# A hand-written issue order rearranged over the first two tiles of a fused window attention and squared-ReLU feed-forward kernel

## The chip, the cores and the metric

The kernel runs on one core of one Trainium2 chip. The metric is the device time of one execution in microseconds (us). Before the change three runs took 849.35, 850.06 and 850.16 us (median 850.06).

## The reference

Eight batches of eight heads, 576 positions each, head size 64. A query sees itself and the 63 positions before it. The result, brought to 4608 tokens of 512 numbers, goes through a two-layer feed-forward block. All of it is float32.

```python
scores = scale * np.matmul(q, k.transpose(0, 1, 3, 2))
mask = (rel >= 0) & (rel < window)          # window = 64
attn = softmax(np.where(mask, scores, -1e9))
x = np.matmul(attn, v)                      # -> (4608, 512)
h = x @ w_in                                # (512, 2048)
r = np.maximum(h, 0.0)
return (r * r) @ w_out                      # (2048, 512)
```

## The kernel before, in words

The 4608 tokens are cut into 12 tiles of 384 tokens. Attention is done in sections: each tile has three sections of four items, an item being a block of 64 queries of four heads. The feed-forward block is done in steps: one step is a tile with one of the 16 blocks of 128 hidden units. Each float32 operand of the feed-forward block is split into a high and a low part, and each product is made of three matmuls (high by high, high by low, low by high).

The first part of the program, through tile 1 and beyond it, is issued in an order that is written out by hand: the string `order`, a list of short tokens. A loop takes token after token and records its instructions; each of the five engines then executes its own instructions in exactly the recorded order and waits with a semaphore where data is missing. So an instruction that waits holds up everything behind it on its engine. After the string, a planner orders the rest; the change does not touch that.

A token is a letter with a number, sometimes with an engine letter behind it (d VectorE, a ScalarE, p GpSimd). The number of an attention token is its section (0 to 2 belong to tile 0, 3 to 5 to tile 1), that of a weight token the weight block, that of a feed-forward token the step. Steps 0 to 4 are tile 0 with weight blocks 0 to 4, steps 5 to 9 are tile 1 with the same blocks. The profile calls TensorE PE, VectorE DVE, ScalarE ACT, GpSimd POOL and SyncE SP.

Loading and turning:
- L, N: DMAs of q and k of batch 0 and 1 (L185). v: DMAs of v (L157). w: two DMAs of one weight block (L104, L105). All are issued by SP, in the order of the tokens. SP has eight completion semaphores in turn, so a DMA is issued only after the one eight places ahead has landed.
- T, U: PE transposes of q and k of batch 0 and 1 (L196). t, u: the copies out of PSUM (L202). U0 to U3 share one PSUM bank, so each waits for the copy of the one before.
- K: matmuls of the identity by itself that nobody reads (L512); K4 is four of them.

Splitting a weight block (two scratch buffers `a`, used in turn):
- a: ScalarE (L118). b: two DVE operations (L120, L121). c: DVE (L123). d: DVE (L125). h: high part, ScalarE (L129). l: low part, DVE (L132). They follow from each other, except that c and d need the weights' words too.

A section of attention, in the order of its dependences:
- S: scores on PE (L235). o: copy on ScalarE (L243). s: masked copy on DVE (L252, L253). z: maximum on DVE (L255). y: its scaling on POOL (L257). e, f: the two halves of the exponentials on ScalarE (L263, four pairs of instructions each). k: a small sum on POOL (L266). R: reciprocal on DVE (L269). m: the multiplication by it on POOL or DVE (L272). X: transposes on PE (L276). x: masked copy on DVE (L280). V: values on PE (L298). H: high part of the result (L313, DVE or ScalarE). Q: low part, DVE (L315).

A feed-forward step:
- M: 12 matmuls (L404). r: ReLU on ScalarE (L413). p: square (L416 on ScalarE). g: high part, ScalarE (L421). G: low part, DVE (L423). O: nine matmuls (L446). All M share one PSUM bank.

M0 needs the three sections of tile 0 (their H and Q) and weight block 0; M5 needs those of tile 1.

Of the kernel before, what the change touches and what calls it, by code (L numbers as in the profile page):

```python
# [29 lines left out]
def window_attention_relu2_ffn(ctx: ExitStack, tc: tile.TileContext, q, k, v, w_in, w_out, out):  # L30
# [457 lines left out]
    order = """
        L0 L1 w0 L2 T0 v0 T1 t0a t1d S0 w1 T2 o0a T3 K5 t2d v1 s0 t3d a0 z0 S1 L3 y0 b0 f0 N0 T4 K3 c0 o1a L4
        t4a s1 T5 K5 e0 w2 d0 t5a N1 k0 z1 h0 S2 R0 y1 v2 m0d e1 l0 X0 K6 o2a x0 a1 v3 s2 V0 f1 b1 H0a k1 T6 K4  # L490
        w3 z2 R1 y2 t6d m1p v4 f2 Q0 T7 X1 c1 t7a U0 e2 x1 S3 u0a k2 d1 V1 o3a T8 v5 H1a R2 s3 m2p t8a T9 a2 Q1
        X2 t9d z3 h1 U2 K2 w4 b2 y3 u2a U1 K4 f3 w5 x2 u1a w6 c2 U3 e3 S4 w7 l1 u3a V2 k3 o4a v6 R3 H2a s4 m3p
        Q2 S5 a3 z4 X3 o5a b3 M0 y4 f4 x3 e4 c3 V3 r0 k4 d2 p0a M1 v7 H3a g0 R4 Q3 m4p h2 s5 X4 r1 G0 p1a z5 O0
        g1 x4 y5 e5 G1 V4 d3 f5 O1 v8 l2 H4a k5 h3 R5 Q4 m5p M2 a4 l3 w8 w9 X5 r2 b4 a5 M3 w10 x5 p2a w11 g2 c4
        r3 V5 w12 p3a G2 g3 w13 d4 O2 w14 G3 h4 H5d O3 w15 l4 q0 Q5 a6 M4 b5 b6 r4 M5 p4a c5 g4 q1 c6 r5 M6 p5a
        G4 g5 d6 O4 r6 d5 h6 G5 p6a M7 h5 g6 l5 O5 r7 G6 a7 l6 p7a O6 b7 g7 a8 G7 M8 c7 b8 O7 r8 p8a d7 g8 M9 G8
        h7 c8 O8 r9 l7 p9a g9 d8 a9 M10 G9 h8 b9 O9 r10 l8 p10a g10 c9 a10 B0 M11 G10 b10 O10 r11 p11a d9 g11 B1
        M12 G11 h9 c10 O11 r12 l9 p12a g12 d10 a11 B2 M13 G12 h10 b11 O12 r13 l10 p13a g13 c11 a12 B3 M14 G13
        b12 O13 r14 p14a d11 g14 B4 M15 G14 h11 c12 O14 r15 l11 p15a g15 d12 a13 B5 M16 G15 h12 b13 O15 r16 l12
        p16a g16 c13 a14 B6 M17 G16 b14 O16 r17 p17a d13 g17 B7 M18 G17 h13 c14 O17 r18 l13 p18a g18 d14 a15 B8  # L500
        M19 G18 h14 b15 O18 r19 l14 p19a g19 c15 B9 M20 G19 D0 O19 r20 p20a d15 q2 g20 M21 G20 h15 D1 O20 r21
        l15 p21a g21 q3 G21 M22 O21 r22 p22d g22 G22 M23 D2 O22 r23 p23d q4 g23 M24 G23 Z22 W22 O23 r24 p24d g24
        G24 S6 M25 o6a D3 q5 s6 O24 r25 z6 p25a y6 g25 f6 G25 S7 O25 e6 o7d s7 v9 k6 z7 M26 R6 y7 m6p f7 D4 X6
        e7 q6 S8 x6 r26 k7 V6 R7 o8a p26d m7p M27 H6a s8 g26 Q6 z8 X7 r27 G26 y8 M28 p27a x7 e8 D5 O26 g27 f8
        G27 q7 V7 r28 k8 R8 p28a m8p S9 g28 H7d M29 G28 Q7 o9d v10 X8 r29 s9 M30 p29a x8 g29 z9 v11 V8 r30 D6 y9
        f9 M31 p30d H8a e9 Q8 O27 k9 R9 m9p G29 O28 g30 r31 p31d X9 G30 g31 O29 x9 D7 G31 M32 O30 r32 p32d g32
        M33 G32 O31 r33 Z31 W31 p33d g33 G33 q8 q9"""
# [586 lines left out]
```

## Time and profile before

| | |
|---|---|
| median of three runs | 850.06 us |
| the profiled execution | 849.04 us, of which the profile's span is 846.9 us |
| PE busy | 828.6 us, 98% of the span |
| DVE busy | 592.3 us, 70% |
| ACT busy | 407.9 us, 48% |
| POOL busy | 182.8 us, 22% |

The span is the time from the first to the last instruction of the profiled execution; all times in rows are counted from its start. A row of the timeline gives an instruction's start, its length, the engine, the line of the kernel, the operation, what it writes and reads, how many were merged, and in brackets the idle time of the engine before it with what ended it. Engines write their results a little later than they can take the next instruction, so neighbouring rows overlap by some 0.1 us on DVE and ACT and by some 0.2 us on PE. A float32 matmul outside the feed-forward block is recorded twice, so four of them show as eight.

### The profile page before, as it was taken

How to read it: one execution, taken by the hardware profiler on the slowest of the kernel's cores; microseconds unless marked ns; L12 is line 12 of the kernel's file. 1: busy time of each engine (PE TensorE's matmuls, PEld its weight loads, DVE VectorE, ACT ScalarE, POOL GpSimd, SP SyncE). 2: the span in 40 equal slices, each digit the busy share in tenths (PEclk: the TensorE clock that was granted, in tenths of full speed). 3: DMA queues.
4: the chain of work that ended last, by engine and by line, in shares of the span. 5: the costliest groups of instructions: out<-in, count | busy, mean ns of one | idle time of the engine just before them, and what ended most of it. 6: DMA issues, size and time to landing. Idle time of an engine off the chain costs nothing.

```text
span 846.9 us, 17709 instructions
## 1 busy us (share of the span) xinstructions
PE 828.6 (98%) x6754; PEld 760.7 (90%) x6754; DVE 592.3 (70%) x889; ACT 407.9 (48%) x1127; POOL 182.8 (22%) x239
## 2 busy tenths in 40 slices
PE   6799999999999999999999999999999999999998
PEld 5688999899999999999999999999999999999997
DVE  5899996656766867867777765688755668544553
ACT  5786874645546554554452354353455324222221
POOL 1220003204557520311230121141112131010110
PEclk9999999999999999999999999999999999999999
DMA  9989966537699884999897786999775555776411
GB/s 216 214 264 359 277 275 117 94 103 175 169 198 265 210 178 112 296 250 209 185 320 247 172 221 158 280 233 264 219 233 154 194 191 180 239 258 212 134 68 74
DMA packets 273011, 173.92 MB, mean 205 GB/s; under 512 B 190496, under 2 KB 239648, under 8 KB 270880
## 3 DMA queue, kind: packets, MB, share of 16 engines
q1 hardware_dynamic: 272928, 172.80, 73.5%
q8 instruction: 53, 0.87, 0.4%
q14 instruction: 30, 0.25, 0.1%
HBM read 138.15 MB, written 34.60 MB: 204 GB/s over the span
## 4 chain that ended last, share of the span: by engine, by line
PE 86%; SPq 4%; DMA 3%; DVE 3%; issue 2%; ACT 1%; POOL 0%; DVEq 0%; POOLq 0%
PE banks L991 29%; PE banks L910 26%; PE banks L446 11%; PE banks L404 11%; PE banks L235 3%; PE banks L298 3%; PE banks L276 2%; DMA w<-in_moe_w_out_dram 1%; SPq L185 1%; DVE a L123 1%; SPq L157 1%; DMA raw<-in_q_dram 1%; DMA w<-in_k_dram 1%; SPq L104 1%; DVE g L423 1%
## 5 line engine op out<-in xcount | busy, mean ns | idle before, releaser
L991 PE MATMUL banks<-w 128*128 128x512 f32 x1152 | 257.5, 380 | 0.0
L991 PEld LDWEIGHTS banks<-w 128*128 128x128 f32 x1152 | 215.7, 189 | 28.4
L404 PE MATMUL banks<-x,w 128*128 128x384 f32 x768 | 137.1, 328 | 1.9 <-ACT r L413 1.4
L446 PE MATMUL banks<-w,g 128*128 128x512 f32 x576 | 136.2, 382 | 0.1
L404 PEld LDWEIGHTS banks<-x,w 128*128 128x128 f32 x768 | 126.6, 189 | 6.1 <-ACT r L413 3.3
L910 PE MATMUL banks<-x,w 128*128 128x384 f32 x768 | 130.3, 326 | 0.0
L936 POOL TENSOR_TENSOR g<-g 128x384 f32<-128x384 f32 x64 | 58.3, 914 | 324.5 <-ACT g L947 309.6
L910 PEld LDWEIGHTS banks<-x,w 128*128 128x128 f32 x768 | 125.6, 189 | 0.0
L446 PEld LDWEIGHTS banks<-w,g 128*128 128x128 f32 x576 | 106.3, 189 | 14.5 <-DVE g L423 1.3
L263 ACT ACTIVATE sel<-sel,nm 128x64 f32<-128x64 f32 x272 | 90.8, 336 | 25.0 <-DVE nm L257 23.1
L910 PE MATMUL banks<-w 128*128 128x384 f32 x576 | 100.7, 329 | 0.0
L999 DVE TENSOR_TENSOR w<-w,banks 128x512 f32<-128x512 f32 x72 | 49.5, 687 | 69.1 <-PE banks L991 68.2
L910 PEld LDWEIGHTS banks<-w 128*128 128x128 f32 x576 | 93.8, 189 | 1.9
L981 ACT CAST w<-w 128x512 fp32r<-128x512 f32 x48 | 29.8, 620 | 72.9 <-PE banks L991 72.9
L413 ACT ACTIVATE r<-banks 128x384 f32<-128x384 f32 x64 | 31.4, 491 | 66.8 <-PE banks L404 66.3
L981 ACT CAST w<-g 128x512 fp32r<-128x512 f32 x48 | 29.7, 621 | 62.1 <-PE banks L991 60.1
L272 POOL TENSOR_TENSOR sel<-sel,nm 128x512 f32<-128x512 f32 x33 | 36.1, 1094 | 107.4 <-ACT g L947 51.7
L263 ACT ACTIVATION_READ_ACCUMULATOR sel<-sel,nm 128x1 f32 x272 | 51.1, 188 | 0.0
L423 DVE TENSOR_TENSOR g<-r,g 128x384 fp32r<-128x384 f32 x64 | 37.5, 586 | 18.0 <-ACT g L421 10.2
L929 DVE SCALAR_TENSOR_TENSOR w<-w 128x384 f32<-128x384 f32 x64 | 47.1, 736 | 1.8
L280 DVE TENSOR_TENSOR pt<-banks,masks 128x1024 f32<-128x1024 f32 x33 | 40.3, 1220 | 10.9 <-PE banks L276 10.9
L535 POOL TENSOR_TENSOR a<-w 128x256 f32<-128x256 f32 x28 | 25.0, 908 | 105.4 <-DVE w L132 79.6
(103 smaller groups left out, 982.1 us busy)
## 6 DMA issues: line engine op xcount, KB each, us to landing
w<-mixed SPq DMA_DIRECT2D x128, 256.0 KB, 5.2
w<-kept SPq DMA_DIRECT2D x64, 512.0 KB, 7.3
w<-kept SPq DMA_DIRECT2D x96, 256.0 KB, 5.9
kept<-w SPq DMA_DIRECT2D x16, 1024.0 KB, 8.5
vt<-in_v_dram SPq DMA_DIRECT2D x144, 64.0 KB, 3.1
w<-in_moe_w_in_dram SPq DMA_DIRECT2D x16, 512.0 KB, 7.5
w<-in_moe_w_out_dram SPq DMA_DIRECT2D x16, 512.0 KB, 8.4
raw<-in_q_dram SPq DMA_DIRECT2D x112, 72.0 KB, 3.2
```

The costliest lines, as they stand in the source:

```text
L263: act.activation(sels[i][:, w, hd], sels[i][:, w, hd], AF.Exp, bias=nms[i][:, n], scale=SCALE, accum_out=sums[i][:, n])
L272: (dve if eng == "d" else pool).tensor_tensor(p, p, rs[i][:, :, None].broadcast_to([P, SW * 2, QB]), ALU.mult)
L280: dve.tensor_tensor(pts[i].rearrange("p (w n) q -> p w n q", n=2), ps_t[i][:, :, None, :].broadcast_to([P, SW, 2, P]), masks.rearrange("p ...
L404: pe.matmul(h_ps, lhsT=weights(kk, part), rhs=in_turn(x[xx][:, kk // 2, kk % 2]), start=n == 0, stop=n == 3 * NK - 1)
L423: dve.tensor_tensor(gs[n][1], rg.pop(n), gs[n][0].bitcast(F32), ALU.subtract)
L446: pe.matmul(acc(t, tb), lhsT=gg[:, ts], rhs=in_turn(weights(part)), start=f == 0 and n == 0, stop=f == NF - 1 and n == 2)
L910: pe.matmul(ps[:, :TT], lhsT=w[:, part, kk * P:(kk + 1) * P], rhs=in_turn(x[:, xx, kk]), start=n < 4 and m == 0, stop=m == 5, skip_group_c ...
L929: plan("dve", 0.57, lambda: dve.scalar_tensor_tensor(x(), x(), 0.0, x(), ALU.max, ALU.mult), [], keys)
L936: plan("pool", 0.95, lambda: pool.tensor_tensor(x(), x(), x(), ALU.mult), [], keys)
L981: plan("act", 0.62, lambda: act.copy(high(c), src()), g_keys, [kh], 0, freed("hi") if new else [])
L991: pe.matmul(ps, lhsT=gg[:, m // 2, m % 2], rhs=in_turn(wo_slot(w[m])[:, part]), start=m == 0 and n == 0, stop=m == 3 and n == 2)
L999: plan("dve", 0.72, lambda: dve.tensor_tensor(by_half(parts(tb)), by_half(parts(tb)), ordered(ps), ALU.add), [key], [kp])
```

## The change

The string `order` is written anew from shortly before the third weight block (w2) is used to shortly before the fourth step. The instructions are the same, with two exceptions: of ten idle matmuls (K4, K2, K4) seven are left (K4, K3), and the high part of section 5 (H5) is made by ScalarE instead of DVE.

```diff
-        t4a s1 T5 K5 e0 w2 d0 t5a N1 ... K6 o2a x0 a1 v3 s2 V0 ...
-        X2 t9d z3 h1 U2 K2 w4 b2 y3 u2a U1 K4 f3 w5 x2 u1a w6 c2 U3 e3 S4 w7 l1 u3a V2 k3 o4a v6 R3 H2a s4 m3p
-        Q2 S5 a3 z4 X3 o5a b3 M0 y4 f4 x3 e4 c3 V3 r0 k4 d2 p0a M1 v7 H3a g0 R4 Q3 m4p h2 s5 X4 r1 G0 p1a z5 O0
...
+        t4a s1 T5 K5 e0 w2 d0 t5a N1 ... K6 o2a x0 a1 w3 s2 V0 ...
+        X2 t9d z3 K3 x2 y3 l1 f3 a2 w4 b2 U2 u2a V2 U1 w5 H2a u1a U3 w6 u3a Q2 S4 w7 c2 o4a d2 M0 a3 s4 z4 r0 e3
+        v6 b3 S5 y4 k3 R3 m3p o5a X3 p0a c3 f4 M1 x3 V3 g0 G0 e4 k4 O0 v7 H3a r1 R4 Q3 h2 m4p s5 X4 p1a l2 z5 g1
...
```

In words: the DMAs of weight block 3 (w3) are issued ahead of those of v3. Ahead of the first operation on weight block 2 (a2 on ScalarE, b2 on DVE) now stand h1 and f3 on ScalarE, x2 and l1 on DVE. V2 moves up to the place right behind U2, and M0 to the place behind S4, ahead of S5 and X3. The other half of the exponentials of section 3, e3, moves down behind r0. x3 and V3 now follow M1 instead of preceding it, and M2 stands ahead of V4 and O1 instead of behind them. l2 moves up from behind d3 to the place ahead of z5; r2 and p2a move up ahead of H4 and a4.

TensorE before, from the wait for batch 1's second load (`w_209` is what N0 and N1 load, `w_354` and `qk_78` are turned q and k, `w_111`, `sel_79` and `pt_80` belong to attention, `x1_318` is tile 0's attention result, `w_248` and `w_433` are the split weight blocks 0 and 1). The rows are U2, K2, U1, K4, U3, V2, S5, X3, M0 and V3:

```order
L196 MATMUL banks_75<-ident_85,w_209 128x64 x4
L512 MATMUL banks_75<-ident_85 128x128 x2
L196 MATMUL banks_75<-ident_85,w_209 128x128 x4
L512 MATMUL banks_75<-ident_85 128x128 x4
L196 MATMUL banks_75<-ident_85,w_209 128x64 x4
L298 MATMUL banks_75<-pt_80,vt_77 64x128 x8
L298 MATMUL banks_75<-pt_80,vt_77 64x64 x16
L235 MATMUL banks_75<-w_354 64x128 x16
L276 MATMUL banks_75<-ident_85,w_111 128x128 x4
L404 MATMUL banks_75<-x1_318,w_248 128x384 x12
L298 MATMUL banks_75<-w_111,vt_77 64x128 x8
```

After the change the same stretch of TensorE, to V3 as well (tile 0's result is now called `x1_317`, weight block 1 `w_426`):

```order
L512 MATMUL banks_75<-ident_85 128x128 x3
L196 MATMUL banks_75<-ident_85,w_209 128x64 x4
L298 MATMUL banks_75<-pt_80,vt_77 64x128 x8
L298 MATMUL banks_75<-pt_80,vt_77 64x64 x16
L196 MATMUL banks_75<-ident_85,w_209 128x128 x4
L196 MATMUL banks_75<-ident_85,w_209 128x64 x4
L404 MATMUL banks_75<-x1_317,w_248 128x384 x12
L235 MATMUL banks_75<-w_354 64x128 x16
L276 MATMUL banks_75<-ident_85,w_111 128x128 x4
L404 MATMUL banks_75<-x1_317,w_426 128x384 x12
L298 MATMUL banks_75<-w_111,vt_77 64x128 x8
```

V2 (`pt_80`) stands right behind U2 and the idle matmuls ahead of it, M0 (`w_248`) stands ahead of S5 and X3, and M1 (`w_426`) stands between X3 and V3. S4 is left out of both pieces.

ScalarE before, over sections 3 and 4. The rows with `w_111` are f3 and e3, those with `w_354` the copies u1, u3, the CAST H2, the L118 row a3 (`w_329` is the raw weight block 3), the row with x8 is f4 and e4 together, L413 is r0:

```order
L263 ACTIVATE w_111,nm_81<-w_111,nm_81 128x64 x4
L202 COPY w_354<-banks_75 128x4x128
L263 ACTIVATE w_111,nm_81<-w_111,nm_81 128x64 x4
L202 COPY w_354<-banks_75 128x4x64
L243 COPY sel_79<-banks_75 128x512
L313 CAST x1_318<-banks_75 128x2x2x128
L118 ACTIVATE a_84<-w_329 128x1024
L243 COPY sel_79<-banks_75 128x512
L263 ACTIVATE sel_79,nm_81<-sel_79,nm_81 128x64 x8
L413 ACTIVATE r_82<-banks_75 128x384
```

ScalarE after, from o4 on (`w_291` is the raw weight block 3): a3, r0, e3, o5, p0 and the first half of section 4's exponentials.

```order
L243 COPY sel_79<-banks_75 128x512
L118 ACTIVATE a_84<-w_291 128x1024
L413 ACTIVATE r_82<-banks_75 128x384
L263 ACTIVATE w_111,nm_81<-w_111,nm_81 128x64 x4
L243 COPY sel_79<-banks_75 128x512
L416 ACTIVATE r_82<-r_82 128x384
L263 ACTIVATE sel_79,nm_81<-sel_79,nm_81 128x64 x4
```

The second half of section 3's exponentials has moved from the place behind u1 to the place behind r0, which reads what M0 wrote.

VectorE before, around section 3's reciprocal (the first L269 row, R3); behind it stand s4 and Q2:

```order
L132 TENSOR_TENSOR w_433<-a_84,w_433 128x2x512
L269 RECIPROCAL nm_81<-nm_81 128x8
L252 COPY_PREDICATED sel_79<-late_90,neg_92 128x2x128
L253 COPY_PREDICATED sel_79<-late_90,banks_75 128x2x128
L315 TENSOR_TENSOR x1_318<-banks_75,x1_318 128x2x2x128
```

VectorE after, around the same reciprocal; behind it stands c3, then x3 (L280) and G0 (L423):

```order
L253 COPY_PREDICATED sel_79<-late_90,banks_75 128x2x128
L255 TENSOR_REDUCE nm_81<-sel_79 128x8
L120 TENSOR_SCALAR a_84<-a_84 128x1024
L121 TENSOR_SCALAR a_84<-a_84 128x1024
L269 RECIPROCAL nm_81<-nm_81 128x8
L123 SCALAR_TENSOR_TENSOR a_84<-w_291,a_84 128x1024
L280 TENSOR_TENSOR w_111<-banks_75,masks_91 128x1024
L423 TENSOR_TENSOR g_83<-r_82,g_83 128x384
```

R3 has moved behind b3, and the neighbour behind it is no longer a masked copy but c3, which reads the weights' words and the scratch buffer, both in SBUF.

More of the change, by code (lines that the diff above doesn't have):

```diff
@@ L489, in window_attention_relu2_ffn @@
         L0 L1 w0 L2 T0 v0 T1 t0a t1d S0 w1 T2 o0a T3 K5 t2d v1 s0 t3d a0 z0 S1 L3 y0 b0 f0 N0 T4 K3 c0 o1a L4
-        t4a s1 T5 K5 e0 w2 d0 t5a N1 k0 z1 h0 S2 R0 y1 v2 m0d e1 l0 X0 K6 o2a x0 a1 v3 s2 V0 f1 b1 H0a k1 T6 K4
-        w3 z2 R1 y2 t6d m1p v4 f2 Q0 T7 X1 c1 t7a U0 e2 x1 S3 u0a k2 d1 V1 o3a T8 v5 H1a R2 s3 m2p t8a T9 a2 Q1
-        X2 t9d z3 h1 U2 K2 w4 b2 y3 u2a U1 K4 f3 w5 x2 u1a w6 c2 U3 e3 S4 w7 l1 u3a V2 k3 o4a v6 R3 H2a s4 m3p
-        Q2 S5 a3 z4 X3 o5a b3 M0 y4 f4 x3 e4 c3 V3 r0 k4 d2 p0a M1 v7 H3a g0 R4 Q3 m4p h2 s5 X4 r1 G0 p1a z5 O0
@@ L494, in window_attention_relu2_ffn @@
[L494 to L507, printed above, removed]
+        t4a s1 T5 K5 e0 w2 d0 t5a N1 k0 z1 h0 S2 R0 y1 v2 m0d e1 l0 X0 K6 o2a x0 a1 w3 s2 V0 f1 b1 H0a k1 T6 K4
@@ new lines, in window_attention_relu2_ffn @@
+        v3 z2 R1 y2 t6d m1p v4 f2 Q0 T7 X1 c1 t7a U0 e2 x1 S3 u0a k2 d1 V1 o3a T8 v5 H1a R2 s3 m2p t8a T9 Q1 h1
+        X2 t9d z3 K3 x2 y3 l1 f3 a2 w4 b2 U2 u2a V2 U1 w5 H2a u1a U3 w6 u3a Q2 S4 w7 c2 o4a d2 M0 a3 s4 z4 r0 e3
+        v6 b3 S5 y4 k3 R3 m3p o5a X3 p0a c3 f4 M1 x3 V3 g0 G0 e4 k4 O0 v7 H3a r1 R4 Q3 h2 m4p s5 X4 p1a l2 z5 g1
+        y5 x4 M2 e5 G1 V4 d3 f5 O1 v8 r2 H4a k5 h3 R5 Q4 m5p p2a a4 l3 g2 w8 w9 X5 b4 a5 M3 w10 x5 G2 w11 c4 r3
+        V5 w12 p3a O2 g3 w13 d4 w14 G3 H5a h4 O3 w15 l4 q0 Q5 a6 M4 b5 b6 r4 M5 p4a c5 g4 q1 c6 r5 M6 p5a G4 g5
@@ new lines, in window_attention_relu2_ffn @@
+        d6 O4 r6 d5 h6 G5 p6a M7 h5 g6 l5 O5 r7 G6 a7 l6 p7a O6 b7 g7 a8 G7 M8 c7 b8 O7 r8 p8a d7 g8 M9 G8 h7 c8
+        O8 r9 l7 p9a g9 d8 a9 M10 G9 h8 b9 O9 r10 l8 p10a g10 c9 a10 B0 M11 G10 b10 O10 r11 p11a d9 g11 B1 M12
+        G11 h9 c10 O11 r12 l9 p12a g12 d10 a11 B2 M13 G12 h10 b11 O12 r13 l10 p13a g13 c11 a12 B3 M14 G13 b12
+        O13 r14 p14a d11 g14 B4 M15 G14 h11 c12 O14 r15 l11 p15a g15 d12 a13 B5 M16 G15 h12 b13 O15 r16 l12 p16a
+        g16 c13 a14 B6 M17 G16 b14 O16 r17 p17a d13 g17 B7 M18 G17 h13 c14 O17 r18 l13 p18a g18 d14 a15 B8 M19
@@ new lines, in window_attention_relu2_ffn @@
+        G18 h14 b15 O18 r19 l14 p19a g19 c15 B9 M20 G19 D0 O19 r20 p20a d15 q2 g20 M21 G20 h15 D1 O20 r21 l15
+        p21a g21 q3 G21 M22 O21 r22 p22d g22 G22 M23 D2 O22 r23 p23d q4 g23 M24 G23 Z22 W22 O23 r24 p24d g24 G24
+        S6 M25 o6a D3 q5 s6 O24 r25 z6 p25a y6 g25 f6 G25 S7 O25 e6 o7d s7 v9 k6 z7 M26 R6 y7 m6p f7 D4 X6 e7 q6
+        S8 x6 r26 k7 V6 R7 o8a p26d m7p M27 H6a s8 g26 Q6 z8 X7 r27 G26 y8 M28 p27a x7 e8 D5 O26 g27 f8 G27 q7
+        V7 r28 k8 R8 p28a m8p S9 g28 H7d M29 G28 Q7 o9d v10 X8 r29 s9 M30 p29a x8 g29 z9 v11 V8 r30 D6 y9 f9 M31
@@ L508, in window_attention_relu2_ffn @@
+        p30d H8a e9 Q8 O27 k9 R9 m9p G29 O28 g30 r31 p31d X9 G30 g31 O29 x9 D7 G31 M32 O30 r32 p32d g32 M33 G32
+        O31 r33 Z31 W31 p33d g33 G33 q8 q9"""
     ps_f = {}
```

## Prediction

> **What bounds the kernel now.** I read first who waited for whom on TensorE (PE), from 66 us to the end (us in total, times, longest).
>
> ```profile
> PE banks L404 <- ACT r L413: 1.2, 2, 0.6
> PE banks L298 <- DVE pt L280: 0.3, 1, 0.3
> ```
>
> These are all the waits in 780 us: behind 66 us PE runs without a hole. So whatever the rearranged stretch does to the start of step 4 (M4, 63.10 below), the end of the program takes over one for one. The stretch itself, in the table by windows (length, then busy us and number of instructions of PE, its weight loads, DVE, ACT and POOL, granted clock, DMA share, GB/s):
>
> ```profile
> 30.00:66.00 36.00, 31.38 (x393) 27.51 (x394) 32.36 (x43) 29.06 (x79) 6.45 (x9) 0.95 0.86 242
> ```
>
> No engine is full here; DVE comes nearest, with 36.00 - 32.36 = 3.64 us idle. What counts is the chain from engine to engine. The timeline of PE shows where it breaks.
>
> ```profile
> 29.91 0.66 PE L276 MATMUL banks<-ident,w 128*128 128x128 f32 x4
> 32.84 0.25 PE L196 MATMUL banks<-ident,w 64*128 64x64 f32 x1 [2.28 <-DVE a L120]
> 33.29 0.40 PE L196 MATMUL banks<-ident,w 64*128 64x64 f32 x3 [0.20 <-DMA w<-in_k_dram]
> 38.28 1.08 PE L298 MATMUL banks<-pt,vt 64*64 64x128 f32 x48
> 40.12 1.10 PE L235 MATMUL banks<-w 64*64 64x128 f32 x32 [0.76 <-ACT x L313]
> 41.15 0.65 PE L276 MATMUL banks<-ident,w 128*128 128x128 f32 x4
> 41.56 2.20 PE L404 MATMUL banks<-x,w 128*128 128x384 f32 x12
> 43.88 1.13 PE L298 MATMUL banks<-w,vt 64*64 64x128 f32 x48
> 63.10 2.11 PE L404 MATMUL banks<-x,w 128*128 128x384 f32 x12
> ```
>
> These are X2, U2 (two rows), V2, S5, X3, M0, V3 and M4. U2 waits 2.28 + 0.20 us for the second load of batch 1. And that hole has a consequence in the granted clock. The windows here follow the 3.41 us pieces in which the clock record changes (columns: length, PE busy, clock, DMA share, GB/s):
>
> ```profile
> 20.28:23.69 3.41, 2.21 (x42) 1.00 1.32 228
> 30.52:33.93 3.41, 0.93 (x7) 1.00 0.87 128
> 33.93:37.34 3.41, 3.41 (x19) 0.50 0.71 199
> ```
>
> A piece with 0.93 us of PE work was followed by one at half clock, a piece with 2.21 us was not. A hole of about 2.5 us can therefore cost a second time.
>
> **The change part by part.** I walk through the new order with the lengths of before.
>
> *The hole at U2 and M0.* N1's loads are issued ahead of w3 and are not moved, so U2 still ends at 33.29 + 0.40 = 33.7. The three idle matmuls fall into the hole. h1, f3, x2 and l1 now run in it too, in front of a2 and b2. Then V2 1.08, the copies H2 and u1, U3, S4. The copies take 0.59 each:
>
> ```profile
> 39.43 0.59 ACT L313 CAST x<-banks 128x512 fp32r<-128x512 f32 x1 [0.32 <-PE banks L298]
> 40.06 1.18 ACT L118 ACTIVATE a<-w 128x1024 f32<-128x1024 f32 x1
> 44.76 0.47 ACT L413 ACTIVATE r<-banks 128x384 f32<-128x384 f32 x1
> 42.09 2.77 ACT sel L263 x16
> ```
>
> 33.7 + 1.08 + 0.59 + 0.59 = 35.95 (U1 hides under H2), U3 about 0.4, S4 about 1.0 like S5's 41.15 - 40.12: M0 starts at 37.3, which is 4.2 us earlier, and ends at 37.3 + 2.1 (M4's row) = 39.4. S5 follows to 40.3. K4 between U1 and U3 is gone; U3 waits for the copy either way. a3 (1.18, the second row) is covered by M0 if w3 has landed at about 38; its two DMAs move ahead of four of the eight v loads on SP's queue, whose issue took
>
> ```profile
> 25.95 8.02 SPq L157 DMA_DIRECT2D vt<-in_v_dram  x8
> 34.02 0.60 SPq L104 DMA_DIRECT2D w<-in_moe_w_in_dram  x1
> ```
>
> so w3 is issued 3 to 5 us sooner than 34.02, behind N1 on the same queue. v3 comes some 2 us later and is read only by V3. I take nothing for either; if w3 were 2 us late, r0 and all behind it would be about 1 us later.
>
> *e3 behind r0.* This is the term that decides. X3 needs section 3's whole chain: e3, k3, R3, m3. Before, that chain was done long before X3, which only waited for its turn behind S5. Now e3 waits on ScalarE behind r0, hence for the end of M0. r0 0.47: 39.4 + 0.45 = 39.8. e3 is half of the fourth row above (e and f of one section): 1.39, 41.2. Then POOL and DVE:
>
> ```profile
> 37.54 0.24 POOL L266 TENSOR_SCALAR nm<-nm 128x8 f32<-128x8 f32 x1 [6.11 <-ACT w L263]
> 45.01 1.27 POOL L266 TENSOR_SCALAR nm<-nm 128x8 f32<-128x8 f32 x1 [2.95 <-ACT sel L263]
> 46.67 1.05 POOL L272 TENSOR_TENSOR sel<-sel,nm 128x512 f32<-128x512 f32 x1 [0.39 <-DVE nm L269]
> ```
>
> ```profile
> 32.12 0.69 DVE L120 TENSOR_SCALAR a<-a 128x1024 f32<-128x1024 f32 x1 [1.01 <-ACT a L118]
> 37.81 0.20 DVE L269 RECIPROCAL nm<-nm 128x8 f32<-128x8 f32 x1 [0.87 <-POOL nm L266]
> 39.15 0.50 DVE L252 COPY_PREDICATED_SCALAR sel<-late,neg 128x256 f32 x1 [1.13 <-ACT sel L243]
> 44.88 1.34 DVE L125 SCALAR_TENSOR_TENSOR a<-w,a 128x1024 int32<-128x1024 int32 x1
> 46.32 0.20 DVE L269 RECIPROCAL nm<-nm 128x8 f32<-128x8 f32 x1
> 46.44 0.64 DVE L315 TENSOR_TENSOR x<-banks,x 128x512 fp32r<-128x512 f32 x1
> 48.08 0.68 DVE L255 TENSOR_REDUCE nm<-sel 128x8 f32<-128x512 f32 x1
> 51.41 1.22 DVE L132 TENSOR_TENSOR w<-a,w 128x1024 fp32r<-128x1024 f32 x1
> 55.16 0.68 DVE L120 TENSOR_SCALAR a<-a 128x1024 f32<-128x1024 f32 x1
> 61.94 1.23 DVE L132 TENSOR_TENSOR w<-a,w 128x1024 fp32r<-128x1024 f32 x1
> ```
>
> k3 0.24, R3 0.20: 41.7 with the hops. m3 starts 0.35 us behind a reciprocal's start (46.32 to 46.67): 41.85, and takes 1.05: X3 at 42.9. That is 42.9 - 41.15 = **1.75 us later** than before, although M0 came 4.2 us earlier, and PE has nothing from 40.3 on. M1 is ready but stands behind X3.
>
> *c3 beside m3.* The same POOL operation took 0.24 us alone and 1.27 us at 45.01, where it ended (46.28) just behind DVE's d operation (44.88 + 1.34 = 46.22). So POOL stood still while DVE read two operands from SBUF. DVE starts its next operation 0.12 us after a reciprocal's start (46.32 to 46.44), POOL 0.35 us after it. Before, a masked copy stood there; now it is c3, which reads two SBUF operands. No row shows m beside c, so its cost is bounded by 0 (alone) and by c3's whole 1.22 us (the length of the L132 row, which has as many elements). I take 0.85 us: c3 ends near 42.85, and the blocked POOL operation gave back some of its length. X3 at 43.75, **2.6 us later**, PE idle for 3.4 us. The Trainium skill (SBUF — State Buffer, "Who interferes with whom") says that a VectorE instruction with two SBUF inputs contends with a GpSimd instruction that reads SBUF and that the later one blocks fully; by that the cost is certain and about 1.1 us.
>
> *From X3 to b4.* Before, 55.16 - 41.15 = 14.0 us. The new chain: X3, M1 and V3 (0.41 + 2.1 + 1.13), about 3.65; H3, r1, h2 and b4's a4 need these rows of ACT:
>
> ```profile
> 45.69 0.57 ACT L313 CAST x<-banks 128x512 fp32r<-128x512 f32 x1
> 46.57 1.04 ACT L129 CAST w<-a 128x1024 fp32r<-128x1024 f32 x1
> 53.20 1.51 ACT L118 ACTIVATE a<-w 128x1024 f32<-128x1024 f32 x1
> 60.86 1.05 ACT L129 CAST w<-a 128x1024 fp32r<-128x1024 f32 x1 [1.11 <-DVE a L125]
> ```
>
> H3 0.57, r1 0.47, h2 1.04: 1.95 with overlaps. l2 1.22, now ahead of z5, and z5 0.68: 1.8. y5 0.3. e5 and f5 2.7. r2, H4, h3, p2 and a4 (0.49 + 0.57 + 1.04 + 0.5 + 1.51, less overlaps): 3.75. Together 14.15: 0.2 us more than before, since l2 got ahead of z5 and r2 and p2 ahead of a4. b4 is 1.95 us later without the collision, 2.8 us with it.
>
> *From b4 to M4.* Before 63.10 - 55.16 = 7.94. Taking H5 off DVE looks like 0.6 us saved, but l4 at 61.94 also waited for h4, which ended at 60.86 + 1.05 = 61.91: nothing.
>
> *The clock.* A hole of 3.4 us is longer than the 2.5 us that cost a half-clock piece before, and behind it stand X3, M1 and V3, 3.65 us of PE work on the chain. 3.41 us at half clock do 1.7 us of work: 1.7 us lost, bounds 0 and 1.7. The half-clock piece of before is contained in before's times, and I walked U1 to S4 at full clock, so nothing is counted twice. I take 1.7, because in the pieces' phase of before (30.52 + 3 x 3.41 = 40.76) the hole fills one of them nearly whole.
>
> **Sum.** 2.8 + 1.7 = 4.5 us on the profiled execution's 849.04 gives 853.5. That execution was 1.0 us faster than the median of 850.06, which I predict from: 850.06 + 4.5 = 854.6.
>
> **The rivals.**
> - *No half clock behind the new hole.* The Trainium skill (TensorE: Matmul & The Clock Gate, "What's actually happening") puts the fall to half after a whole idle window of about 3.4 us; that was not needed here, since the piece at 30.52 held 0.93 us of work. But in another phase of the pieces a hole of 3.4 us could split. Then 850.06 + 2.8 = 852.9. Chance 0.20. If c3 doesn't block m3 either: 850.06 + 1.95 = 852.0. Chance 0.04.
> - *The clock falls behind both holes.* The hole at U2 stays, shortened by three idle matmuls to some 1.7 us; with U2 and V2 the piece would hold about 1.5 us of work, between 0.93 and 2.21. V2, U1, U3 and S4 would run at half clock, partly under the copies: about 1.0 us, 855.6. Chance 0.13.
> - *Faster: DVE is what binds.* Its waits before a2's result, R3 and s4 (1.01 + 0.87 + 1.13 = 3.0) vanish because x2 and l1 fill the first and M0 covers the others; PE's hole at X3 is then only time that PE would have waited elsewhere. 850.06 - 3.0 = 847.1. It decides this way if X3 starts before 41.15. The ACT order speaks against it: e3 can't start before M0's end. Chance 0.07.
> - *No change.* Later holes take up the shift. Against it: 1.5 us of waits in all behind 66 us. 850.1, chance 0.06.
>
> **How the numbers follow.** The forecast (collision and one half-clock piece) has the remaining 0.50. The low end is the rival with neither, 852.0; the high end the one with two pieces plus 0.8 us, the spread of the three runs: 856.4. This leaves out the cases of faster and no change, 0.13, and little else. A measurement of this kernel can tell 0.2%, 1.7 us, from no change. Slower by more: 0.50 + 0.20 + 0.04 + 0.13 = 0.87; within it 0.06; faster 0.07.
>
> **What would show it.** In the profile of the changed kernel: M0 near 37.3; X3 near 43.75 with an idle time of PE of 3 us or more ahead of it, released by POOL's L272; that L272 about 2 us long, with DVE's L123 beside it; a half-clock piece near 44 to 48; M4 near 67.6. X3 before 41.2 would make the prediction wrong at its root; M4 near 65 would leave out the clock or the collision; a wait of PE behind 66 us that is gone would mean that the shift is not handed on one for one.

## The result and the profile after

The changed kernel takes 854.4 us, median of six runs (852.92 to 856.62). The kernel before took 849.55 us in six runs beside it (847.05 to 850.16). The ratio is 1.0064, with a 95% interval of 1.0044 to 1.0085: 4.85 us slower, where 4.5 were predicted.

The profiled execution took 856.62 us, 7.58 more than the profiled one of before; it was the slowest of the six. TensorE's timeline, with the rows that answer to those of before (U2, V2, M0, S5, X3, M1, M4):

```profile
35.13 0.74 PE L196 MATMUL banks<-ident,w 64*128 64x64 f32 x4 [0.98 <-DMA w<-in_q_dram]
35.88 1.43 PE L298 MATMUL banks<-pt,vt 64*64 64x128 f32 x48
...
39.79 2.22 PE L404 MATMUL banks<-x,w 128*128 128x384 f32 x12
42.53 1.10 PE L235 MATMUL banks<-w 64*64 64x128 f32 x32 [0.53 <-ACT r L413]
46.85 0.90 PE L276 MATMUL banks<-ident,w 128*128 128x128 f32 x4 [3.21 <-POOL w L272]
47.40 3.73 PE L404 MATMUL banks<-x,w 128*128 128x384 f32 x12
...
70.43 2.15 PE L404 MATMUL banks<-x,w 128*128 128x384 f32 x12
```

U2 begins at 35.13 instead of 32.84. That is 2.29 us of the 7.58, and it is not the change: batch 1's second load was issued and landed later in this execution (SP issued it from 27.21 us on instead of 24.63), and on SP's queue it stands ahead of everything that moved. (Across all executions of this study U2 ended between 31.1 and 35.9, whatever the kernel.) So the stretch is measured from U2. From U2's start to M4's it took 63.10 - 32.84 = 30.26 us before and 70.43 - 35.13 = 35.30 now: **5.04 us more**. From M4's start to the start of the last matmul it is 779.87 now and 779.64 before. Of PE's waits behind 66 us the first two rows are the ones of before, and the third is new and 0.2 us:

```profile
PE banks L404 <- ACT r L413: 1.2, 2, 0.6
PE banks L298 <- DVE pt L280: 0.3, 1, 0.3
PE banks L446 <- DVE g L423: 0.2, 1, 0.2
```

The shift is handed on one for one. In the stretch itself X3 now has a wait of 3.21 us, which it did not have before, released by POOL's L272, that is by m3. The chain up to it on ScalarE (a3, r0, the first of e3's four pieces), on VectorE (the second half of b3, R3, c3) and on POOL (k3, m3):

```profile
40.41 1.65 ACT L118 ACTIVATE a<-w 128x1024 f32<-128x1024 f32 x1
42.04 0.49 ACT L413 ACTIVATE r<-banks 128x384 f32<-128x384 f32 x1
42.43 0.34 ACT L263 ACTIVATE w<-w,nm 128x64 f32<-128x64 f32 x1
```

```profile
43.74 0.69 DVE L121 TENSOR_SCALAR a<-a 128x1024 int32<-128x1024 int32 x1
44.56 0.20 DVE L269 RECIPROCAL nm<-nm 128x8 f32<-128x8 f32 x1
44.68 1.22 DVE L123 SCALAR_TENSOR_TENSOR a<-w,a 128x1024 int32<-128x1024 int32 x1
```

```profile
44.00 0.52 POOL L266 TENSOR_SCALAR nm<-nm 128x8 f32<-128x8 f32 x1 [0.21 <-ACT w L263]
44.85 1.95 POOL L272 TENSOR_TENSOR w<-w,nm 128x512 f32<-128x512 f32 x1 [0.32 <-DVE nm L269]
```

m3 begins at 44.85, while c3 runs until 44.68 + 1.22 = 45.90, and takes 1.95 us instead of 1.04 or 1.05. It ends 0.90 us behind c3, so all but 0.14 us of its work was done after c3 had ended.

The granted clock in the pieces of 3.41 us around the hole, and the stretch from 30 to 66 us as a whole (same columns as before):

```profile
30.00:66.00 36.00, 27.61 (x427) 23.60 (x422) 27.44 (x38) 26.86 (x79) 7.71 (x11) 0.95 0.82 219
...
40.31:43.72 3.41, 2.80 (x43) 2.29 (x41) 3.36 (x5) 3.41 (x11) 0.53 (x1) 1.00 0.36 81
43.72:47.13 3.41, 0.28 (x3) 0.28 (x4) 2.03 (x3) 3.41 (x18) 2.55 (x3) 1.00 0.88 264
47.13:50.54 3.41, 3.41 (x14) 3.41 (x13) 1.80 (x3) 0.68 (x5) 1.03 (x2) 0.50 1.01 366
```

VectorE is idle 36.00 - 27.44 = 8.6 us of the 36, against 3.6 before: no engine has become full. The piece with the hole holds 0.28 us of PE work, and the next one is granted half the clock: M1 takes 3.73 instead of 2.2 us.

### The profile page after: what moved, and what is told of

Same layout as the page of the kernel before. It is cut to its first block, busy times and chain, and to the rows that moved or that the text cites. A ratio compares the mean times of both kernels' runs of the same rounds, so it can differ in the third digit from the quotient of the medians.

```text
span 854.5 us, 17699 instructions
## 1 busy us (share of the span) xinstructions
PE 830.8 (97%) x6748; PEld 761.5 (89%) x6748; DVE 591.7 (69%) x888; ACT 407.6 (48%) x1128; POOL 183.7 (22%) x239
## 4 chain that ended last, share of the span: by engine, by line
PE 86%; SPq 5%; DVE 3%; DMA 2%; ACT 2%; issue 2%; POOL 0%; DVEq 0%; POOLq 0%
PE banks L991 29%; PE banks L910 26%; PE banks L446 11%; PE banks L404 11%; PE banks L235 3%; PE banks L298 3%; PE banks L276 2%; SPq L147 2%; SPq L185 1%; DMA w<-in_moe_w_out_dram 1%; SPq L157 1%; DMA w<-in_k_dram 1%; DVE a L123 1%; DVE a L125 1%; SPq L105 1%
## 5 line engine op out<-in xcount | busy, mean ns | idle before, releaser
L413 ACT ACTIVATE r<-banks 128x384 f32<-128x384 f32 x64 | 31.3, 488 | 66.1 <-PE banks L404 64.4
L272 POOL TENSOR_TENSOR sel<-sel,nm 128x512 f32<-128x512 f32 x33 | 36.1, 1093 | 108.6 <-ACT g L947 51.7
L423 DVE TENSOR_TENSOR g<-r,g 128x384 fp32r<-128x384 f32 x64 | 37.7, 589 | 18.0 <-ACT g L421 9.7
L280 DVE TENSOR_TENSOR pt<-banks,masks 128x1024 f32<-128x1024 f32 x33 | 40.3, 1220 | 11.1 <-PE banks L276 11.1
```

The lines of the kernel that those rows point to most:

```text
L272: (dve if eng == "d" else pool).tensor_tensor(p, p, rs[i][:, :, None].broadcast_to([P, SW * 2, QB]), ALU.mult)
L280: dve.tensor_tensor(pts[i].rearrange("p (w n) q -> p w n q", n=2), ps_t[i][:, :, None, :].broadcast_to([P, SW, 2, P]), masks.rearrange("p ...
L423: dve.tensor_tensor(gs[n][1], rg.pop(n), gs[n][0].bitcast(F32), ALU.subtract)
```

## The experiments

The steps of the stretch, in us, from each kernel's profile. "U2 end" is where batch 1 has been turned; in e2, e3 and e10 the loads came early and V2 then waited for other data, so there the first two columns say less than the others. The last column is the time at half clock between U2's end and X3, and between X3 and M4.

| kernel | U2 end to M0 | U2 end to X3 | M0 to X3 | X3 to b4 | b4 to M4 | m3 | half clock |
|---|---|---|---|---|---|---|---|
| before | 7.88 | 7.47 | | 14.00 | 7.94 | 1.04 | 3.4, 0 |
| before again (e9) | 7.87 | 7.46 | | 13.98 | 7.93 | 1.04 | 3.4, 0 |
| changed | 3.92 | 10.99 | 7.07 | 15.69 | 7.89 | 1.95 | 0, 3.4 |
| changed again (e5) | 5.80 | 13.45 | 7.65 | 15.65 | 7.89 | 1.95 | 6.8, 3.4 |
| e1 chain of section 3 early | 5.92 | 9.84 | 3.92 | 14.35 | 7.88 | 1.04 | 6.8, 0 |
| e2 c3 later | 5.03 | 11.26 | 6.23 | 15.65 | 7.89 | 1.04 | 0, 3.4 |
| e3 hole filled | 5.18 | 12.28 | 7.10 | 14.02 | 7.88 | 1.95 | 0, 0 |
| e4 M1 ahead of X3 | 6.02 | 14.61 | 8.59 | 14.29 | 7.89 | 2.06 | 9.5, 3.4 |
| e6 old tail | 5.32 | 12.10 | 6.78 | 12.90 | 7.75 | 1.95 | 3.4, 0 |
| e7 best | 3.85 | 7.76 | 3.91 | 13.35 | 7.75 | 1.04 | 0, 0 |
| e8 front part alone | 9.48 | 8.71 | | 14.51 | 7.79 | 1.04 | 7.5, 2.8 |
| e10 more idle matmuls | 4.28 | 11.40 | 7.12 | 15.72 | 7.89 | 1.95 | 0, 3.4 |
| e11 H5 on VectorE | 5.01 | 11.78 | 6.77 | 15.64 | 7.89 | 1.95 | 2.9, 3.4 |

From M4 to the last matmul all of them took 779.4 to 779.9 us.

### The chain of section 3 ahead of M0

```diff
-u1a U3 w6
+u1a e3 U3 w6
-o4a d2 M0
+o4a d2 k3 R3 m3p M0
-r0 e3 v6 b3 S5 y4 k3 R3 m3p o5a
+r0 v6 b3 S5 y4 o5a
```

> Changed kernel with section 3's chain moved up: e3 into ScalarE's gap behind u1, and k3, R3, m3 ahead of M0, so that X3 has its operand before S5 ends. The gauge is the time from U2's first matmul to M4's in the profile: 30.26 us in the kernel before, 35.30 us in the changed one. Theory A (the wait of X3 for e3's chain, and the half-clock piece behind it, are the loss): the hole of 3.2 us in front of X3 and the 1.5 us of M1's slow half go, gauge about 30.6, time about as before. Rival B (M4 is set by VectorE's sum of work and later waits, the hole at X3 only shows): gauge above 33.

Measured: 850.59 us (849.17 to 852.87, ten runs) against 848.05; ratio 1.0030, interval 1.0019 to 1.0042. TensorE's timeline around X3 (S5, X3, M1):

```profile
41.17 1.10 PE L235 MATMUL banks<-w 64*64 64x128 f32 x32
42.21 0.66 PE L276 MATMUL banks<-ident,w 128*128 128x128 f32 x4
42.62 2.20 PE L404 MATMUL banks<-x,w 128*128 128x384 f32 x12
```

No row has a wait: X3 follows S5 at once, 3.92 us behind M0 instead of 7.07, m3 is 1.04 us long and M1 runs at full clock. So the hole, the blocked m3 and the half-clock piece behind it all come from where e3 and its followers stand. What is left of the loss is not the chain: 2.5 us in the medians. The forecast for the stretch was missed: from U2's first matmul to M4 it is 33.93 us, not 30.6, which is the side of rival B. From U2's end it is 32.07 us, against 29.41 before and 34.57 in the changed kernel. Part of the rest, in this execution, is the clock behind U2, which I had only as a rival:

```profile
29.62:33.03 3.41, 2.11 (x29) 1.70 (x31) 3.09 (x4) 2.36 (x10) 0.24 (x1) 1.00 1.22 242
33.03:36.44 3.41, 2.73 (x50) 2.21 (x40) 2.71 (x4) 1.98 (x7) 0.00 (x0) 0.50 0.92 227
36.44:39.85 3.41, 3.41 (x41) 3.18 (x41) 2.74 (x5) 2.71 (x10) 1.72 (x2) 0.50 0.37 82
```

A piece with 2.11 us of PE work is followed by two at half clock, and M0 begins 5.92 us behind U2's end. In e7 below, where no piece fell, it is 3.85: the two pieces cost 2.07 us. That is most of the 2.66 us by which the stretch from U2's end is still longer than before, so the miss is for the most part the clock's and does not speak for rival B.

### c3 out of m3's way

```diff
-X3 p0a c3 f4 M1 x3 V3
+X3 p0a f4 M1 x3 c3 V3
```

> Changed kernel with c3 moved on VectorE from behind R3 to behind x3, so that no operation with two SBUF operands runs beside m3. Theory A (c3 blocks m3): m3 takes 1.04 us instead of 1.95, X3 comes 0.9 us sooner, the hole is 2.3 us; gauge 34.4 if the clock still falls, 32.9 if it does not. Rival (m3 is slow for another reason, or the 0.9 us are lost again because c3 is later): m3 1.95, or gauge 35.3.

Measured: 851.85 us (one run). VectorE (R3, x3, c3), and m3 on POOL:

```profile
41.02 0.20 DVE L269 RECIPROCAL nm<-nm 128x8 f32<-128x8 f32 x1
43.10 1.22 DVE L280 TENSOR_TENSOR w<-banks,masks 128x1024 f32<-128x1024 f32 x1 [1.88 <-PE banks L276]
44.24 1.22 DVE L123 SCALAR_TENSOR_TENSOR a<-w,a 128x1024 int32<-128x1024 int32 x1
```

```profile
41.31 1.04 POOL L272 TENSOR_TENSOR w<-w,nm 128x512 f32<-128x512 f32 x1 [0.32 <-DVE nm L269]
```

With VectorE idle beside it m3 takes 1.04 us, and X3 comes 6.23 us behind M0 instead of 7.07: 0.84 less. From M0 to M4 it is 29.77 us instead of 30.65. The c3 term is shown, with its size: 0.91 us of m3, of which 0.84 to 0.88 reach X3 and M4. From U2's first matmul to M4 it is 35.39 us, where 34.4 was expected: V2 (0.64 us, for its load) and U1 (0.47 us) waited ahead of M0, which c3 has no part in. The half-clock piece stayed (43.7 to 47.1), with a hole of 2.31 us.

### The hole filled with idle matmuls

```diff
-R3 m3p o5a X3
+R3 m3p o5a K12 X3
```

> Changed kernel with 12 idle matmuls (2.9 us) behind S5, in the hole ahead of X3. Nothing else moves. Theory A (the hole causes the half-clock piece): no half-clock piece behind it, M1 takes 2.2 us instead of 3.73, gauge 33.8. Rival (the half clock comes from elsewhere, or what M1 loses is waited for later anyhow): gauge 35.3.

Measured: 852.13 us (one run). TensorE: the idle matmuls, X3, M1 and M4.

```profile
40.95 2.94 PE L513 MATMUL banks<-ident 128*128 128x128 f32 x24
44.23 0.66 PE L276 MATMUL banks<-ident,w 128*128 128x128 f32 x4 [0.34 <-POOL w L272]
44.65 2.20 PE L404 MATMUL banks<-x,w 128*128 128x384 f32 x12
...
66.13 2.15 PE L404 MATMUL banks<-x,w 128*128 128x384 f32 x12
```

X3 comes as late as in the changed kernel (7.10 us behind M0; 7.07 there), so the matmuls themselves moved nothing. But M1 takes 2.20 us, no piece behind X3 is at half clock, and X3 to M4 takes 66.13 - 44.23 = 21.90 us instead of 70.43 - 46.85 = 23.58. The clock term is **1.68 us**. And X3 to b4 is 14.02, against 14.00 before the change: apart from the clock this part got no longer. From U2's first matmul to M4 it is 34.64 us and not the expected 33.8, since V2 and U1 waited 1.2 us ahead of M0.

### M1 ahead of X3

```diff
-R3 m3p o5a X3 p0a c3 f4 M1 x3 V3
+R3 m3p o5a M1 X3 p0a c3 f4 x3 V3
```

> Changed kernel with M1 ahead of X3 on TensorE, so that the hole holds M1. X3 comes as late as before (m3 is not moved), V3 follows x3. Theory A (the work standing behind X3 is what the hole costs): no half-clock piece, V3 about 2.4 us sooner, gauge about 32.9. Rival B (M4 is set by VectorE and ScalarE behind section 4): gauge near 35.

Measured: 855.55 us (one run). X3 still waited 1.49 us for m3, and V3 behind it 1.32 us for x3. Four half-clock pieces lay in the stretch in this execution (31.9 to 42.1 and 49.0 to 52.4), so its time says nothing on the order. From U2's first matmul to M4 it is 38.67 us, more than either theory had. This one is inconclusive.

### The changed kernel once more

> The changed kernel itself once more, beside the next three on the same chip, because the first profiles came from chips on which the loads of the first 30 us landed up to 2.9 us apart. The gauge is now X2's first matmul to M4's: 33.2 us in the kernel before, 37.6 us in the changed one. All theories: m3 near 1.95 us, X3 about 14 us behind X2, gauge 36 to 38 depending on the number of half-clock pieces (about 1.65 us each), time 4 us above the kernel before.

Measured: 853.87 us (853.16 to 856.25, four runs) against 848.21; ratio 1.0068, interval 1.0044 to 1.0092. The profiled execution was the slowest, 856.25 us. Its clock, from the piece with U2 to the one behind X3:

```profile
30.93:34.34 3.41, 1.75 (x30) 1.30 (x32) 2.79 (x4) 2.74 (x10) 0.24 (x1) 0.99 1.10 252
34.34:37.75 3.41, 2.73 (x44) 2.17 (x36) 2.74 (x4) 1.17 (x2) 0.00 (x0) 0.50 0.81 210
37.75:41.16 3.41, 3.41 (x40) 3.22 (x39) 2.50 (x5) 2.00 (x3) 0.00 (x0) 0.51 0.37 82
...
44.57:47.98 3.41, 1.02 (x8) 1.02 (x9) 1.66 (x3) 3.41 (x18) 2.01 (x2) 0.99 1.04 366
47.98:51.40 3.42, 3.42 (x20) 2.98 (x21) 1.47 (x3) 0.22 (x2) 1.28 (x2) 0.51 1.06 384
```

The same kernel, but here the clock falls behind both holes. From U2's end to M4 it took 36.99 us, 2.42 more than in the other profile of the changed kernel (34.57), all of it ahead of X3. The expected 14 us from X2 to X3 and 36 to 38 us from X2 to M4 were missed (16.95 and 40.49), and m3 was as expected (1.95).

### The old order behind s5

```diff
-s5 X4 p1a l2 z5 g1 y5 x4 M2 e5 G1 V4 d3 f5 O1 v8 r2 H4a k5 h3 R5 Q4 m5p p2a a4 l3 g2 ...
+s5 X4 p1a z5 g1 x4 y5 e5 G1 V4 d3 f5 O1 v8 l2 H4a k5 h3 R5 Q4 m5p M2 a4 l3 ...
-w13 d4 w14 G3 H5a h4
+w13 d4 O2 w14 G3 h4 H5d
```

> Changed kernel, but from section 5's s on in the order of the kernel before: l2 back behind d3, M2 behind H4 and Q4, r2 and p2a back behind a4, H5 on VectorE. The late e3 stays. As the prediction priced it (this tail costs 0.2 us): gauge X2 to M4 37.4. Rival C (behind the late X3 the new tail costs more: l2's 1.22 us stand in front of z5 and so of e5 and f5, r2 and p2a's 0.9 us in front of H4, h3 and a4, while the old tail had room there): gauge 35.5, time about 2 us below the changed kernel.

Measured: 853.28 us (852.74 to 853.62, four runs); ratio 1.0056, interval 1.0034 to 1.0077, against 1.0068 of the changed kernel: the times don't separate the two. The profiles do. X3 and M4 are here:

```profile
46.43 0.66 PE L276 MATMUL banks<-ident,w 128*128 128x128 f32 x4 [3.53 <-POOL w L272]
...
67.08 2.11 PE L404 MATMUL banks<-x,w 128*128 128x384 f32 x12
```

Here b4 (the L120) starts on VectorE right behind l3, in the changed kernel (the second fence) it waits for a4:

```profile
57.61 1.80 DVE L132 TENSOR_TENSOR w<-a,w 128x1024 fp32r<-128x1024 f32 x1
59.33 0.68 DVE L120 TENSOR_SCALAR a<-a 128x1024 f32<-128x1024 f32 x1
```

```profile
62.54 0.69 DVE L120 TENSOR_SCALAR a<-a 128x1024 f32<-128x1024 f32 x1 [0.33 <-ACT a L118]
```

X3 to M4 is 20.65 us with the old tail and 21.90 with the new one (e3, also without a half-clock piece). So the old tail is 1.25 us shorter behind a late X3 than the new one. Its edits were not tried one by one; in the changed kernel's profile it is a4, behind r2 and p2a on ScalarE, that b4 waits for. Both forecasts were missed: X2 to M4 is 36.69 us, between the 37.4 of the prediction's price and rival C's 35.5, with a half-clock piece ahead of M0 that the first profile of the changed kernel did not have, and the median is 0.6 us below that of the changed kernel and not 2.

### The best of both

e1's edits, e6's edits, x3 right behind X3 as before the change, and eight idle matmuls instead of three around U2.

```diff
-z3 K3 x2 ... u1a e3 U3
+z3 K5 x2 ... u1a e3 K3 U3
-X3 p0a c3 f4 M1 x3 V3
+X3 x3 p0a c3 f4 M1 V3
```

> The parts that the runs speak for together: the changed kernel's work in front of the third weights and M0 ahead of S5, section 3's chain moved up as in the first experiment, x3 right behind X3 on VectorE, the old tail, and five idle matmuls in the wait for N1 and three between U1 and U3, to keep the clock. Theory A with C (late chain, clock and tail are all of the loss): gauge X2 to M4 31.5 to 32.5, time 1 to 1.7 us below the kernel before. Rival B (VectorE's sum of work sets M4): gauge 33 or more, no faster than the kernel before.

Measured: 848.41 us (847.33 to 851.91, twelve runs) against 848.21; ratio 1.0003, interval 0.999 to 1.0016. It is not to be told from the kernel before, and 5.5 us faster than the changed one. TensorE's timeline (M0, S5, X3, M1, M4):

```profile
38.12 2.22 PE L404 MATMUL banks<-x,w 128*128 128x384 f32 x12
41.00 1.10 PE L235 MATMUL banks<-w 64*64 64x128 f32 x32 [0.66 <-DVE sel L253]
42.03 0.66 PE L276 MATMUL banks<-ident,w 128*128 128x128 f32 x4
42.45 2.20 PE L404 MATMUL banks<-x,w 128*128 128x384 f32 x12
...
63.13 2.11 PE L404 MATMUL banks<-x,w 128*128 128x384 f32 x12
```

M0 stands 4 us earlier than in the kernel before, and nothing waits for m3. Yet X3 is not earlier: 7.76 us behind U2's end (7.47 before), since S5 waits for section 4's masked copy on VectorE. From U2's end to M4 it is 63.13 - 34.27 = 28.86 us against 29.4: half a microsecond gained, which the timing can't show. From X2 to M4 it is 31.92 us, as theory A with C had it, but the 1 to 1.7 us that it expected in the time did not come. This version with the early M0 is worth no more than that.

### The front part alone, on the kernel before

```diff
-t8a T9 a2 Q1 X2 t9d z3 h1 U2 K2 w4 b2 y3 u2a U1 K4 f3 w5 x2 u1a w6 c2 U3 e3 S4 w7 l1 u3a V2 k3 o4a v6 R3 H2a
-s4 m3p Q2 S5
+t8a T9 Q1 h1 X2 t9d z3 K3 x2 y3 l1 f3 a2 w4 b2 U2 u2a V2 U1 w5 H2a u1a e3 w6 c2 U3 S4 w7 u3a k3 o4a v6 R3
+s4 m3p Q2 S5
```

> The kernel before with the first part of the change alone: h1, f3, x2 and l1 ahead of a2 and b2, V2 behind U2, three idle matmuls in the wait for N1, e3 behind u1; M0 stays behind X3 and everything behind S5 is as before. If the work in front of the third weights is a gain by itself (VectorE waited 1.01 us there, TensorE held K4 between U1 and U3): gauge X2 to M4 about 32, time about 1.2 us below the kernel before. Rival (the wait for N1 sets this stretch whatever stands in it): gauge 33.2, same time.

Measured: 849.36 us (847.59 to 850.69, ten runs); ratio 1.0008, interval 0.9994 to 1.0022: no difference that can be told. In the profiled execution three pieces were at half clock, 34.0 to 44.3, and S5 waited 1.66 us for the same masked copy of section 4 as in e7. X2 to M4 is 34.19 us, longer than either theory had. So this part of the change brings, by itself, nothing that can be measured; whether it would without the half-clock pieces stays open.

### The kernel before once more

> The kernel before, once more with a profile. Theory A (the clock falls behind the wait at U2 in every execution of this order, as in the first profile): a half-clock piece of 3.41 us begins between U2 and M0, X2 to X3 is 11.2 to 11.4 us, X2 to M4 33.1 to 33.3. Theory B (whether it falls depends on the phase of the pieces and on how late the second load of batch 1 lands, here as in the new orders): no piece or two of them in the stretch; X2 to M4 then is some 1.7 us less or more per piece, as far as the wait at M0 doesn't cover it, so anywhere from 32 to 35 us. From M4 to the last matmul 779.4 to 779.9 by both.

Measured: 847.03 us (one run). U2 in two parts, X3 and M4:

```profile
30.17 0.27 PE L196 MATMUL banks<-ident,w 64*128 64x64 f32 x1
31.38 0.40 PE L196 MATMUL banks<-ident,w 64*128 64x64 f32 x3 [0.94 <-DMA w<-in_k_dram]
...
39.23 0.66 PE L276 MATMUL banks<-ident,w 128*128 128x128 f32 x4
...
61.14 2.11 PE L404 MATMUL banks<-x,w 128*128 128x384 f32 x12
```

From U2's end (31.78) to X3 it is 7.46 us and to M4 29.36; in the first profile 7.47 and 29.41. The load landed two microseconds earlier, the half-clock piece began at 32.2 instead of 33.9, and the stretch is the same to 0.05 us. So for the kernel before what is said of the stretch from U2's end on doesn't hang on one execution. Counted from X2 both forecasts of theory A were missed (9.72 us to X3 and 31.63 to M4), as U2 waited 0.94 us here and not 2.48. The row of U2 in the first profile names VectorE's L120 as the end of its wait; here U2 begins at 30.17, ahead of that L120 (30.62), so that operation is not what U2 waits for, and the load remains.

### More idle matmuls around U2, in the changed kernel

```diff
-z3 K3 x2
+z3 K5 x2
-H2a u1a U3
+H2a u1a K3 U3
```

> The changed kernel with five idle matmuls instead of three ahead of U2 and three more between U1 and U3; nothing else. Theory A (the fall of the clock behind U2, which took 2.1 to 2.4 us up to M0 in four of the new orders, comes from the idle matmuls that the change took out): no half-clock piece between X2 and M0, X2 to M0 6.9 to 7.0 us; X3 stays late (X2 to X3 13.9 to 14.1, m3 1.95) and the piece behind the hole at X3 stays, X2 to M4 37.5; the median is 0.5 to 2 us under that of the changed kernel, 852 to 853.5. Theory B (the phase of the pieces alone decides): some executions still have X2 to M0 near 9.1, and the median stays at 853.5 to 854.5.

Measured: 852.96 us (852.66 to 854.01, four runs) against 848.36; ratio 1.0059, interval 1.0043 to 1.0076. The profiled execution had no half-clock piece ahead of X3, and M0 came 6.89 us behind X2, as theory A had it; X3 (14.01) and M4 (37.62) came as it had them too. M0 is here:

```profile
36.15 2.22 PE L404 MATMUL banks<-x,w 128*128 128x384 f32 x12
```

The median lies 0.9 us under that of the changed kernel in e5 and its slowest run 2.2 us under, as it should if the fall behind U2 is gone; but the intervals of the two ratios overlap, the two were run on different chips, and it is one profile; three of the eight profiles of the changed order with its three idle matmuls had no such fall either. I call it likely, not shown.

### H5 back on VectorE

```diff
-w14 G3 H5a h4
+w14 G3 h4 H5d
```

> The changed kernel with the high part of section 5 on VectorE as before; nothing else. Theory A (the prediction's: between b4 and M4 VectorE is not what ends last, since l4 waits for h4 on ScalarE): from b4's start to M4's start 7.9 us as in both profiles, no change within 0.15 us. Theory B (VectorE binds there, and taking H5 off it is worth its 0.6 us): 8.4 to 8.6 us.

Measured: 855.6 us (one run). VectorE (b4, H5, l4):

```profile
61.83 0.69 DVE L120 TENSOR_SCALAR a<-a 128x1024 f32<-128x1024 f32 x1 [0.34 <-ACT a L118]
...
67.97 0.68 DVE L313 CAST x<-banks 128x512 fp32r<-128x512 f32 x1
68.76 1.23 DVE L132 TENSOR_TENSOR w<-a,w 128x1024 fp32r<-128x1024 f32 x1
```

b4 to M4 is 7.89 us, to a hundredth what it is with H5 on ScalarE. There VectorE has no H5, and l4 waits 0.65 us for h4 instead. The whole time is no evidence on H5: this execution had a half-clock piece ahead of X3 and another behind it.

## Why the prediction was right

854.6 us was predicted and 854.4 measured, and the chain of causes is the one given. That the two agree to 0.2 us is luck: the kernel before has a median of 849.55 over six runs and not 850.06, and the loss is 4.85 us and not 4.5. Step by step, with the steps counted from U2's start in the two first profiles:

- **The hole at U2 and M0.** Predicted 4.2 us earlier, measured 4.06 (4.66 us behind U2's start instead of 8.72). S5's 0.53 us of waiting for r0, which the walk didn't have, cost nothing, since X3 came later anyway. Nor did w3 ahead of v3, taken as nothing: a3 and V3 begin without a wait in the profile.
- **X3, the deciding term.** Predicted 2.6 us later, measured 3.41 (11.72 instead of 8.31). Direction and mechanism held: e1 moves the chain and the wait is gone. The size was 0.8 us short. 0.2 of it is M0's own place. The other 0.6 lies between M0's start and X3, 7.06 us instead of the walk's 43.75 - 37.3 = 6.45: e3 began 2.64 us behind M0's start and not 2.5 (M0 ran 2.22 us, and a3 held ScalarE until 42.06); k3 and R3 took 0.35 more, since b3's L121 ran on VectorE until 44.43, beside which k3 took 0.52 us instead of 0.24 (in e2, e3 and e10, where the two also overlap, 0.56 to 0.59; in e4, e5, e6 and e11, where L121 had ended before, 0.24); and m3 with c3 beside it 0.1 more. I had looked for VectorE's neighbour of m3 only, not for that of k3.
- **c3 beside m3.** Taken as 0.85 us between bounds of 0 and 1.22; m3 grew by 0.91, and e2 gets 0.84 of it back at X3. The Trainium skill (SBUF — State Buffer, "Who interferes with whom") has it that the later of the two instructions is blocked; the trace agrees but for 0.14 us, since m3, begun 0.17 us behind c3, ended 0.90 us behind c3's end and takes 1.04 alone. By the walk's own times (c3's end at 42.84, m3's start at 41.85) full blocking would cost 1.0 us and not the 1.1 that the prediction gives for it.
- **X3 to b4.** Predicted 14.15 at full clock, measured 14.02 in e3, and term by term the walk holds there (H3 3.74 us behind X3, l2 5.69, e5 7.87, a4's end 13.99, where the walk has 3.65, 5.6, 7.7 and 14.15). Not seen was that the old tail would have used the late X3 (12.90 in e6), so 1.1 to 1.25 us of the result do belong to the new tail as a whole, where the prediction put 0.2 us on the moves of l2, r2 and p2a. The sum was not touched, because it was made against before's 14.0.
- **b4 to M4.** Predicted unchanged at 7.94 with H5 off VectorE; 7.89 with it there and with it away (e11).
- **The clock.** Predicted 1.7 us behind the new hole, measured 1.68 (e3 against the changed kernel; X3 to b4 is 15.64 to 15.72 in the five profiles with this order and the piece there, and 14.02 without it). The half-clock piece was expected near 44 to 48 and was at 47.13 to 50.54, in an execution that ran 2.3 us later.
- **The shift is handed on.** 779.4 to 779.9 us from M4 to the end in every run.

The terms add up in the profiled execution: 3.41 at X3, 1.68 from X3 to b4, -0.05 to M4: 5.04. They are those of one execution. The other profile of the changed kernel lost 36.99 - 29.41 = 7.58 us from U2's end to M4, and both were the slowest runs of their sets; what the run of median time is made of was not seen.

The rival *no half clock behind the new hole* had a chance of 0.20. In five of the six profiles in which the changed order's hole stands unfilled (the changed kernel twice, e2, e10, e11) the clock fell. It did not in e6, where the hole of 3.53 us was split over two pieces with 1.74 and 1.56 us of PE work, the way that the rival describes. The rival *clock falls behind both holes* had 0.13 and 855.6 us, and this chance was too low. It was in the second profile of the changed kernel (two pieces behind U2, 856.25 us) and in e11 (one, 855.6 us). Behind U2 the clock fell in five of the eight profiles with the change's three idle matmuls there and M0 moved up (e1, e4, e5, e6, e11; not in the first of the changed kernel, e2, e3). So it is no rare case, and it costs 2.4 us rather than 1.0 where two pieces fall; with one piece X3 came 0.8 us (e11) and 1.1 us (e6) later behind U2's end than in the first profile, near the estimate. The rivals on the other side failed at the point that was named for them: X3 did not start before 41.15 (it came 3.41 us later, counted from U2), and no later hole took up the shift.

What stays open is how often the clock falls behind U2 in either order, and whether e10's matmuls prevent it always; that needs many profiles and not one of each.

## What to carry to other kernels

Moving work forward on the engine that looks idle gains only if what stands behind it on that engine isn't made later: here TensorE's M0 came 4 us earlier, but the exponentials that X3 needs had been put behind what reads M0, and the next ready matmuls stood behind X3. In a hand-written order, follow the last input of each instruction on the bottleneck engine through all engines (here ScalarE, POOL, VectorE, POOL), and look at each step for the neighbour on another engine beside which it takes longer (m3 took 1.95 us beside c3 and 1.04 alone). Fill holes that must stay with idle matmuls (1.68 us here). And measure a stretch from the event that starts it: from U2's end to M4 two executions of the kernel before agree to 0.05 us, while the loads ahead of it vary by more than the effect. The changed kernel's two differ by 2.42 us even so, through the clock.
